# Decoding with a cached 32-head attention and an MLP: wq and wo read as 64 KB rows, x and the heads' results spread over partitions to match, and release signals passed on by waits

## The chip, the cores and the metric

The kernel runs on one core of a Trainium2 chip. Its time is the device time in microseconds of one execution; the number that counts is the median of the runs shown. A profile of one execution is read beside it.

## The reference

One token passes through grouped-query attention over a cache of 65,536 keys and through an MLP, side by side, on the same normalised input. All arrays are float32.

```python
x: (1, 1, 512)   k_cache, v_cache: (1, 8, 65536, 128)
wq: (512, 4096)  wo: (4096, 512)  w1: (512, 1792)  w2: (1792, 512)

xn = layernorm(x)
q = (xn @ wq) as 32 heads of 128          # 4 query heads to each of 8 k/v heads
p = softmax(q @ k.T * 128 ** -0.5)        # over all 65,536 keys
attention = (p @ v) joined @ wo
mlp = relu(xn @ w1) @ w2
return x + attention + mlp
```

The caches hold 268 MB each; wq and wo 8.4 MB each; w1 and w2 3.7 MB each.

## The kernel before, in words

The engines' programs are written out by hand: each engine runs its own list in order, and they meet at semaphores. `Flow.op` waits for the marks it is given, issues an instruction and counts it. Nothing reorders the work.

**Loads.** SyncE issues all large loads on its queue, in this order: wq in two halves of 4 MB (line 149), then for each of 40 steps one part of k (line 158) and one part of v (line 161), then w1 and w2 (lines 164 and 165), then, after the sums over wq, wo in six pieces into the same buffer `big` (lines 268 to 283). There is one buffer for k and one for v. A step is one k/v head and one of five parts of its keys (`PART`: 7, 7, 6, 6 and 6 tiles of 2048 keys). The load of the next k waits until `k_free` has counted the step before, the load of the next v for `v_free`. wq lies in memory head group by head group, so that a partition receives four rows of 8 KB from each half; a piece of wo likewise consists of rows of 8 KB or less. What goes through the helper `load` stands under its line, 142, in the profile. ScalarE issues two small loads on its own queue: x as `xT` (128 rows of 16 B) and x as `x4` (four rows of 512 B).

**Start.** VectorE and TensorE compute the mean and variance and make `xn`. `columns` (line 234) multiplies weights by `xn`: matmuls with one column of weights each, four of them on four groups of 32 rows; VectorE copies the result to `rows`, TensorE transposes it in four blocks, and VectorE picks the columns needed. It runs twice for q, once for each half of wq, and once for the MLP. GpSimd copies one head group's q into `qcur` (line 290) and raises `q_in`.

**A step.** TensorE scores the seven tiles of k into two pairs of PSUM banks `pa` and `pb` (line 307; the seventh tile is also scored where the part has six, and not used). VectorE transposes two tiles at a time into `tr` (line 336); after all of them it drains and raises `k_free` (line 343). Then the maximum, its spread by small matmuls (lines 312 to 314) and `bias`; ScalarE's exponentials into `wt` (line 384); TensorE's 28 matmuls over v into `acc_o` (line 323); and VectorE's addition into `acc`, which raises `v_free` when it is done (lines 357 to 363). The loops of TensorE, VectorE and ScalarE are hardware loops (`Fori`); `head_slot` gives the place in a block of loaded instructions at which a loop's first instruction lies.

**End.** The MLP's first layer, its 14 matmuls over w2 into `acc_z` (line 412), the heads' totals, and the eight matmuls of line 436 that turn the heads' results into `oT`, copied at line 441. Column j of `oT` is head j over its 128 positions, and slice j of `big` is the 128 x 512 piece of wo for that head. 24 slices are summed into `acc_z`, which is copied (line 451) and folded into `acc_y` (line 454); the last eight slices go to `acc_y` in four column blocks (line 463), as their loads arrive. VectorE adds x, and SyncE stores y.

Of the kernel before, what the change touches and what calls it, by code (L numbers as in the profile page):

```python
# [10 lines left out]
ALU = mybir.AluOpType  # L11
AX = mybir.AxisListType
# [9 lines left out]
CT = 4  # L22
# [11 lines left out]
HALF = HKV // 2  # L34
A = D // P
FB = DFF // P
WO = [(0, 4), (4, 2), (6, 1)]
LAST = [(0, 2), (2, 1), (3, 1)]
DIRECT = 6
# [29 lines left out]
def attention_and_mlp_kernel(  # L69
# [21 lines left out]

    nc = tc.nc
# [15 lines left out]
    x4 = place("x4", P)  # L108
    st = place("st", 8)
# [23 lines left out]
    with tc.tile_critical():  # L133
# [6 lines left out]
        def load(engine, name, dst, src, n=16):  # L140
# [6 lines left out]
        tq = big.rearrange("p (h f) -> p h f", h=HKV)  # L147
        wq_in = [
            load(sy, f"wq{i}", tq[:, i : i + HALF, :], wq[i : i + HALF].rearrange("h p a f -> p h (a f)"))
            for i in range(0, HKV, HALF)  # L150
        ]
# [78 lines left out]
        )  # L230
        DV.op(lambda e: e.memset(idg, 1.0))
        DV.op(lambda e: e.tensor_copy(idg[:, :G], ident[:G, :G]), DV.mark)

        def columns(weights, widths, marks, relu=False):


            pr, pt = pa[:, 0, :], pb[:, 0, :]
            DV.op(lambda e: e.memset(pr, 0.0), PE.mark)
            for a in range(A):
                for c, n in enumerate(widths):  # L240
                    PE.op(
                        lambda e: e.matmul(  # L242
                            pr[32 * c : 32 * c + 1, :n], xn[:, a : a + 1], weights(c, a),
                            start=(a == 0), stop=(a == A - 1),
                        ),
                        DV.mark, xn_in, *marks,
                    )
            if relu:
                DV.op(lambda e: e.tensor_scalar_max(rows, pr, 0.0), PE.mark)
            else:  # L250
                DV.op(lambda e: e.tensor_copy(rows, pr), PE.mark)
            for j in range(4):
                PE.op(
                    lambda e: e.transpose(pt[:, j * P : (j + 1) * P], rows[:, j * P : (j + 1) * P], ident),
                    DV.mark, made,
                )
            return pt.rearrange("p (j c l) -> p c j l", j=4, c=CT)[:, :, :, 0]

        for i in range(0, HKV, CT):
            w = tq[:, i : i + CT, :].rearrange("p h (a f) -> p h a f", a=A)  # L260
            q = columns(lambda c, a: w[:, c, a, :], [512] * CT, [wq_in[i // HALF]])
            DV.op(lambda e: e.tensor_copy(qall[:, i : i + CT, :], q), PE.mark)
        q_made, wq_read = DV.mark, PE.mark
# [5 lines left out]
        to = big  # L269
        parts = []  # L270
        wo_in = []
        for h, n in WO:
            mark = load(
                sy, f"wo{h}", to[:, h * 2048 : (h + n) * 2048].rearrange("p (h f) -> p h f", f=2048),
                wo[h : h + n].rearrange("h p g f -> p h (g f)"),
            )
            wo_in += [mark] * (n * G)
        for g, n in LAST:
            at = (HKV - 1) * 2048 + g * D
            mark = load(  # L280
                sy, f"wl{g}", to[:, at : at + n * D], wo[HKV - 1, :, g : g + n, :].rearrange("p g f -> p (g f)")
            )
            wo_in += [mark] * n
# [48 lines left out]
        with nc.Fori(0, HKV, engines=[ENG.DVE], head_slot={ENG.DVE: 0}):  # L332
            for n, nt in enumerate(PART):
                for s in range(0, MOST, 2):
                    w = min(2, MOST - s)
                    i = ve.transpose(  # L336
# [3 lines left out]
                    if s < 4:  # L340
                        i.then_inc(s_dve, 1)
                ve.sem_inc(s_tiles, -4)
                ve.drain().then_inc(k_free, 1)  # L343
# [11 lines left out]
                flat = acc.rearrange("p b d -> p (b d)")  # L355
                if n == 0:
                    i = ve.tensor_copy(flat, acc_o)  # L357
                else:
                    ve.wait_ge(s_alpha, 1).then_inc(s_alpha, -1)
                    i = ve.scalar_tensor_tensor(  # L360
                        flat, flat, alpha[:, n : n + 1], acc_o, op0=ALU.mult, op1=ALU.add
                    )
                i._wait_ge(s_o, 1).then_inc(v_free, 1)
# [13 lines left out]
        with nc.Fori(0, HKV, engines=[ENG.Activation], head_slot={ENG.Activation: 0}):  # L377
# [24 lines left out]
        ends = [min(DFF, 512 * (c + 1)) for c in range(CT)]  # L402
        hid = columns(
            lambda c, a: w[:, a, 512 * c : ends[c]], [ends[c] - 512 * c for c in range(CT)], [w1_in], relu=True
        )
# [35 lines left out]
        oT_in = DV.op(lambda e: e.tensor_copy(oT, pm[:, P : P + HQ]), PE.mark)  # L441

        for j in range(HQ):
            h, g = divmod(j, G)
            row = to[:, j * D : (j + 1) * D]
            lhsT = oT[:, j : j + 1]
            if h < DIRECT:
                gather(g, lhsT, row, [oT_in, wo_in[j]], last=(h == DIRECT - 1))
                if j == DIRECT * G - 1:
# [10 lines left out]
            else:  # L460
                for c in range(CT):
# [3 lines left out]
                            start=False, stop=(j == HQ - 1),  # L465
                        ),
                        oT_in, wo_in[j],
# [34 lines left out]
```

## Time and profile before

| | us |
|---|---|
| median of 3 runs | 1311.38 (1307.83 to 1313.49) |
| the profiled execution, its own time | 1308.58 |
| its span, first to last instruction | 1306.8 |
| TensorE busy | 748.4 |
| VectorE busy | 294.9 |
| ScalarE busy | 88.3 |
| DMA queue of SyncE, share of 16 engines | 99.6% |
| bytes moved | 561.09 MB, 429 GB/s over the span |

Mean granted clock of TensorE: 0.735 of full speed. A busy share is time in which an engine had an instruction under way; loads and their issue are not part of it. "PE", "DVE", "ACT", "POOL" and "SP" are TensorE, VectorE, ScalarE, GpSimd and SyncE; "PEld" is the loading of a matmul's weights. Packets in a DMA queue are the pieces that one DMA engine moves at a time. A float32 matmul leaves two records.

### The profile page before, as it was taken

The page shows a single profiled execution, that of the slowest core. Times are in us where ns is not written, and L with a number is a line of the kernel's source. Part 1 is how long each engine was busy: PE and PEld are TensorE (multiplying, and loading weights), DVE is VectorE, ACT ScalarE, POOL GpSimd, SP SyncE. Part 2 cuts the span into 40 slices and gives each one's busy share as a digit, 9 for nine tenths or more (in the row PEclk, how much of TensorE's full clock was granted, in tenths as well). Part 3 has the DMA queues.
Part 4 walks back from the last instruction along what each step waited for, and adds up shares of the span by engine and source line. Part 5 has one row for each costly group of instructions (what it writes and reads, how often), then busy time and mean ns, then how long its engine had stood idle before and what let it go on. Part 6 is the DMA issues. An engine that isn't in the chain of part 4 may idle for free. (4 is left out here: it accounts for less than half of the span.)

```text
span 1306.8 us, 11612 instructions
## 1 busy us (share of the span) xinstructions
PE 748.4 (57%) x4958; PEld 214.8 (16%) x4958; DVE 294.9 (23%) x474; ACT 88.3 (7%) x372; POOL 4.6 (0%) x22
## 2 busy tenths in 40 slices
PE   4456555556555655556655655556655656555666
PEld 1111111111111111111111111111111111111112
DVE  2122222222212222222222222222221232222221
ACT  0000000000000001000000000000000000100000
POOL 0000000000000000000000000000000000000000
PEclk9667777777767777777766777777766777777778
DMA  9999999999999999999999999999999999999998
GB/s 397 446 427 412 429 433 437 430 427 432 433 435 432 432 436 432 435 429 433 428 441 432 433 433 428 441 425 433 433 435 441 425 433 437 429 442 429 432 425 353
DMA packets 14408, 561.09 MB, mean 429 GB/s; under 512 B 1592, under 2 KB 1600, under 8 KB 1984
## 3 DMA queue, kind: packets, MB, share of 16 engines
q1 hardware_dynamic: 14248, 561.00, 99.6%
q8 instruction: 3, 0.05, 0.0%
q14 instruction: 5, 0.04, 0.0%
q10 hardware_dynamic: 152, 0.00, 0.0%
HBM read 560.99 MB, written 0.00 MB: 429 GB/s over the span
## 5 line engine op out<-in xcount | busy, mean ns | idle before, releaser
L323 PE MATMUL acc_o<-vs,wt 128*16 128x512 f32 x2240 | 328.5, 750 | 128.6 <-PEq L319 128.6
L307 PE MATMUL pa<-ks,qcur 128*32 128x512 f32 x1280 | 220.1, 820 | 285.8 <-PEq L302 285.8
L336 DVE STREAM_TRANSPOSE tr<-pa 128x1024 f32<-128x1024 f32 x80 | 100.0, 1250 | 404.2 <-PE pa L307 404.2
L307 PE MATMUL pb<-ks,qcur 128*32 128x512 f32 x960 | 139.3, 685 | 0.0
L323 PEld LDWEIGHTS acc_o<-vs,wt 128*16 128x16 f32 x2240 | 76.4, 114 | 347.2 <-issue 347.2
L384 ACT ACTIVATE wt<-tr,bias 128x96 f32<-128x96 f32 (+1 forms) x160 | 73.1, 465 | 875.5 <-ACTq L379 875.5
L307 PEld LDWEIGHTS pa<-ks,qcur 128*32 128x32 f32 x1280 | 48.6, 134 | 420.0 <-issue 409.1
L360 DVE SCALAR_TENSOR_TENSOR acc<-acc,alpha,acc_o 128x512 f32<-128x512 f32 x32 | 23.9, 747 | 348.8 <-PE acc_o L323 348.8
L336 DVE STREAM_TRANSPOSE tr<-pb 128x1024 f32<-128x1024 f32 x80 | 76.9, 962 | 38.0 <-PE pb L307 38.0
L312 PE MATMUL pm<-ident,m 128*4 128x128 f32 x40 | 11.5, 286 | 90.0 <-DVE m L348 73.0
L307 PEld LDWEIGHTS pb<-ks,qcur 128*32 128x32 f32 x960 | 41.2, 138 | 110.5 <-issue 86.6
L313 PE MATMUL pm<-dg,ones 4*128 4x4 f32 x80 | 21.6, 338 | 26.7 <-DVE dg L352 26.7
L384 ACT ACTIVATION_READ_ACCUMULATOR wt<-tr,bias 128x1 f32 x160 | 29.9, 187 | 0.0
L357 DVE COPY acc<-acc_o 128x512 f32<-128x512 f32 x8 | 5.5, 691 | 102.9 <-PE acc_o L323 102.9
L345 DVE TENSOR_REDUCE mc<-tr 128x4 f32<-128x384 f32 (+1 forms) x32 | 26.2, 819 | 3.7
L312 PEld LDWEIGHTS pm<-ident,m 128*4 128x4 f32 x40 | 3.3, 81 | 126.3 <-DVE m L348 102.0
L313 PEld LDWEIGHTS pm<-dg,ones 4*128 4x128 f32 x80 | 18.1, 280 | 34.9 <-DVE dg L352 34.9
L314 PE MATMUL pm<-dg,rowg 4*128 4x1 f32 x80 | 21.6, 337 | 0.0
L314 PEld LDWEIGHTS pm<-dg,rowg 4*128 4x128 f32 x80 | 20.6, 313 | 0.0
L382 ACT COPY wt<-zero 128x64 f32<-128x64 f32 x8 | 2.0, 244 | 232.5 <-ACTq L379 232.5
L242 PE MATMUL pa<-big,xn 128*1 128x512 f32 x64 | 11.5, 888 | 10.0 <-DMA big<-wq 10.0
L353 DVE COPY bias<-pm 128x5 f32<-128x5 f32 x40 | 6.5, 164 | 41.5 <-PE pm L314 41.5
(83 smaller groups left out, 115.3 us busy)
## 6 DMA issues: line engine op xcount, KB each, us to landing
ks<-k SPq DMA_DIRECT2D x24, 6144.0 KB, 19.8
vs<-v SPq DMA_DIRECT2D x24, 6144.0 KB, 19.4
ks<-k SPq DMA_DIRECT2D x16, 7168.0 KB, 23.5
vs<-v SPq DMA_DIRECT2D x16, 7168.0 KB, 24.3
big<-wq SPq DMA_DIRECT2D x2, 4096.0 KB, 17.2
ks<-w SPq DMA_DIRECT2D x2, 3584.0 KB, 17.7
big<-wo SPq DMA_DIRECT2D x1, 4096.0 KB, 31.4
big<-wo SPq DMA_DIRECT2D x1, 2048.0 KB, 35.9
```

Of the source, the lines that this page charges most:

```text
L242: lambda e: e.matmul(pr[32 * c : 32 * c + 1, :n], xn[:, a : a + 1], weights(c, a), start=(a == 0), stop=(a == A - 1),),
L307: i = te.matmul(pt[32 * c : 32 * c + 32, :], qcur, ks[:, at : at + TW], start=True, stop=True)
L312: te.transpose(pm[:G, :P], m, ident)._wait_ge(s_dve, 3).then_inc(s_max, 1)
L313: te.matmul(pm[:, P : P + G], ones[:G, :], dg[:, :G], start=True, stop=True)._wait_ge(s_dve, 4)
L314: te.matmul(pm[:, P + G : P + G + 1], rowg, dg[:, G : G + 1], start=True, stop=True).then_inc(s_max, 1)
L323: mm = te.matmul(acc_o[32 * c : 32 * c + WIDE * G, :], wt[:, i * WIDE : (i + 1) * WIDE, :].rearrange("p b g -> p (b g)"), vs[:, i * 512 : ...
L336: i = ve.transpose(tr[:, s * SUB : (s + w) * SUB, :].rearrange("p b i -> p (b i)"), (pa, pb)[s // 2 % 2][:, :w, :].rearrange("p i k -> p ( ...
L345: i = ve.reduce_max(top, tr[:, : nt * SUB, :G].rearrange("p b g -> p g b"), axis=AX.X)
L353: ve.tensor_copy(bias[:, n, :], pm[:, P : P + G + 1])._wait_ge(s_max, 2).then_inc(s_bias, 1)
L357: i = ve.tensor_copy(flat, acc_o)
L360: i = ve.scalar_tensor_tensor(flat, flat, alpha[:, n : n + 1], acc_o, op0=ALU.mult, op1=ALU.add)
L384: i = se.activation(wt[:, : nt * SUB, g], tr[:, : nt * SUB, g], AF.Exp, bias=bias[:, n, g : g + 1], scale=scale, accum_out=part[:, n, g : ...
```

## The change

- wq is read in one load: partition p receives the 64 KB that lie at p times 64 KB. Its 128 partitions are then 8 head groups times 16 row blocks, and a slice of `big` holds, for partition (h, i), row `(i, r)` of head group h. For this x is loaded a second time as `xr`, by ScalarE's queue: 32 values of x in each partition, the same 16 blocks for each of 8 head groups. VectorE normalises `xr` and multiplies it by `mine`, which is 1 where a partition belongs to a head group, giving `xs` with eight columns to each slice (in `tr`'s memory). 32 matmuls with eight columns of weights follow in one go; after the four transposes one reduction makes `qall` for all heads.
- wo is read in the same order, as pieces of 16, 8, 4, 2, 1 and 1 slices of a 64 KB row. Behind `oT`, VectorE makes `pick` (in `tr`'s memory), eight matmuls spread `oT` over the partitions, and a product with `mine` and a reduction give `sw`, whose column j goes with slice j.
- `k_free` is raised by a wait of VectorE for `s_tiles`, once the tiles are scored that the following k load will overwrite; `v_free` by a wait for `s_o`, ahead of the addition into `acc`.
- The loops' heads lie at slot 128 (VectorE) and 68 (ScalarE); TensorE's stays at 0.

```diff
--- before.py
+++ after.py
@@ -31,12 +31,12 @@
 NP = len(PART)
 STEPS = HKV * NP
 WIDE = 4
-HALF = HKV // 2
 A = D // P
 FB = DFF // P
-WO = [(0, 4), (4, 2), (6, 1)]
-LAST = [(0, 2), (2, 1), (3, 1)]
-DIRECT = 6
+R = HKV
+SLICES = R * G
+WO = [16, 8, 4, 2, 1, 1]
+DIRECT = 24
 EPS = 1e-5
 
 
...
@@ -106,6 +110,13 @@
     wt = place("wt", MOST * SUB, G)
     xT, xc, sq, xn = (place(n, A) for n in ("xT", "xc", "sq", "xn"))
     x4 = place("x4", P)
+    xr, sw = place("xr", SLICES), place("sw", SLICES)
+    mine = place("mine", HKV)
+
+    flat_tr = tr.rearrange("p b i -> p (b i)")
+    xs = flat_tr[:, : SLICES * HKV].rearrange("p (i h) -> p i h", h=HKV)
+    pick = flat_tr[:, : R * P].rearrange("p (r q) -> p r q", r=R)
+    spread = flat_tr[:, R * P : R * (P + HQ)].rearrange("p (r h g) -> p r h g", r=R, h=HKV)
     st = place("st", 8)
     ident, ones = place("ident", P), place("ones", P)
     sel, selb, selg = place("sel", WIDE, G), place("selb", WIDE), place("selg", G)
@@ -144,11 +155,10 @@
 
 
         x_in = load(se, "x_in", xT, x.rearrange("(p a) -> p a", p=P))
-        tq = big.rearrange("p (h f) -> p h f", h=HKV)
-        wq_in = [
-            load(sy, f"wq{i}", tq[:, i : i + HALF, :], wq[i : i + HALF].rearrange("h p a f -> p h (a f)"))
-            for i in range(0, HKV, HALF)
-        ]
+        wq_in = load(sy, "wq_in", big, wq.rearrange("h (i r) a f -> (h i) (r a f)", r=R))
+        xr_in = load(
+            se, "xr_in", xr, x.rearrange("(i j) -> i j", j=SLICES).unsqueeze(0).to_broadcast([HKV, P // R, SLICES])
+        )
         for i in range(STEPS):
             h, n = divmod(i, NP)
             lo, nt = sum(PART[:n]), PART[n]
@@ -228,59 +238,58 @@
                 rowg.rearrange("g (i j) -> g i j", j=G), ident[:G, :G].unsqueeze(1).to_broadcast([G, P // G, G])
             )
         )
+        DV.op(lambda e: e.reduce_sum(mine, ident.rearrange("p (h i) -> p h i", h=HKV), axis=AX.X))
+        DV.op(lambda e: e.tensor_scalar(xr, xr, st[:, 1:2], None, op0=ALU.subtract), xr_in)
+        DV.op(lambda e: e.tensor_scalar_mul(xr, xr, st[:, 7:8]), DV.mark)
+        xs_in = DV.op(
+            lambda e: e.tensor_mul(
+                xs, xr.unsqueeze(2).to_broadcast([P, SLICES, HKV]),
+                mine.unsqueeze(1).to_broadcast([P, SLICES, HKV]),
+            ),
+            DV.mark,
+        )
         DV.op(lambda e: e.memset(idg, 1.0))
         DV.op(lambda e: e.tensor_copy(idg[:, :G], ident[:G, :G]), DV.mark)
 
-        def columns(weights, widths, marks, relu=False):
-
-
-            pr, pt = pa[:, 0, :], pb[:, 0, :]
-            DV.op(lambda e: e.memset(pr, 0.0), PE.mark)
-            for a in range(A):
-                for c, n in enumerate(widths):
-                    PE.op(
-                        lambda e: e.matmul(
-                            pr[32 * c : 32 * c + 1, :n], xn[:, a : a + 1], weights(c, a),
-                            start=(a == 0), stop=(a == A - 1),
-                        ),
-                        DV.mark, xn_in, *marks,
-                    )
-            if relu:
-                DV.op(lambda e: e.tensor_scalar_max(rows, pr, 0.0), PE.mark)
-            else:
-                DV.op(lambda e: e.tensor_copy(rows, pr), PE.mark)
+        pr, pt = pa[:, 0, :], pb[:, 0, :]
+
+        def clear():
+            return DV.op(lambda e: e.memset(pr, 0.0), PE.mark)
+
+        def turn():
+
             for j in range(4):
                 PE.op(
                     lambda e: e.transpose(pt[:, j * P : (j + 1) * P], rows[:, j * P : (j + 1) * P], ident),
                     DV.mark, made,
                 )
-            return pt.rearrange("p (j c l) -> p c j l", j=4, c=CT)[:, :, :, 0]
-
-        for i in range(0, HKV, CT):
-            w = tq[:, i : i + CT, :].rearrange("p h (a f) -> p h a f", a=A)
-            q = columns(lambda c, a: w[:, c, a, :], [512] * CT, [wq_in[i // HALF]])
-            DV.op(lambda e: e.tensor_copy(qall[:, i : i + CT, :], q), PE.mark)
-        q_made, wq_read = DV.mark, PE.mark
+            return pt.rearrange("p (j c l) -> p j c l", j=4, c=CT)
+
+        cleared = clear()
+        for i in range(SLICES):
+            c = i % CT
+            PE.op(
+                lambda e: e.matmul(
+                    pr[32 * c : 32 * c + HKV, :], xs[:, i, :], big[:, i * 512 : (i + 1) * 512],
+                    start=(i < CT), stop=(i >= SLICES - CT),
+                ),
+                cleared, xs_in, wq_in,
+            )
+        wq_read = PE.mark
+        DV.op(lambda e: e.tensor_copy(rows, pr), PE.mark)
+        q = turn()[:, :, :, :HKV].rearrange("p j c h -> p h j c")
+        DV.op(lambda e: e.reduce_sum(qall, q, axis=AX.X), PE.mark)
+        q_made = DV.mark
         PE.need(DV.mark)
         AC.need(DV.mark)
 
 
         sy.wait_ge(*wq_read)
-        to = big
-        parts = []
         wo_in = []
-        for h, n in WO:
-            mark = load(
-                sy, f"wo{h}", to[:, h * 2048 : (h + n) * 2048].rearrange("p (h f) -> p h f", f=2048),
-                wo[h : h + n].rearrange("h p g f -> p h (g f)"),
-            )
-            wo_in += [mark] * (n * G)
-        for g, n in LAST:
-            at = (HKV - 1) * 2048 + g * D
-            mark = load(
-                sy, f"wl{g}", to[:, at : at + n * D], wo[HKV - 1, :, g : g + n, :].rearrange("p g f -> p (g f)")
-            )
-            wo_in += [mark] * n
+        flat_wo = wo.rearrange("h (i r) g f -> (h i) (r g f)", r=R)
+        for n in WO:
+            cut = slice(len(wo_in) * D, (len(wo_in) + n) * D)
+            wo_in += [load(sy, f"wo{len(wo_in)}", big[:, cut], flat_wo[:, cut])] * n
 
 
         ge.wait_ge(*q_made)
@@ -329,18 +338,24 @@
             mm.then_inc(s_o, 1)
 
 
-        with nc.Fori(0, HKV, engines=[ENG.DVE], head_slot={ENG.DVE: 0}):
+        with nc.Fori(0, HKV, engines=[ENG.DVE], head_slot={ENG.DVE: 128}):
             for n, nt in enumerate(PART):
+
+                follow = PART[(n + 1) % NP]
                 for s in range(0, MOST, 2):
                     w = min(2, MOST - s)
+                    if s < follow <= s + 2 and follow == MOST:
+                        ve.wait_ge(s_tiles, s // 2 + 1).then_inc(k_free, 1)
                     i = ve.transpose(
                         tr[:, s * SUB : (s + w) * SUB, :].rearrange("p b i -> p (b i)"),
                         (pa, pb)[s // 2 % 2][:, :w, :].rearrange("p i k -> p (i k)"),
                     )._wait_ge(s_tiles, s // 2 + 1)
                     if s < 4:
                         i.then_inc(s_dve, 1)
+                    if s < follow <= s + 2 and follow < MOST:
+                        ve.wait_ge(s_tiles, s // 2 + 1).then_inc(k_free, 1)
                 ve.sem_inc(s_tiles, -4)
-                ve.drain().then_inc(k_free, 1)
+                ve.drain()
                 top = m if n == 0 else mc
                 i = ve.reduce_max(top, tr[:, : nt * SUB, :G].rearrange("p b g -> p g b"), axis=AX.X)
                 if n:
@@ -353,14 +368,15 @@
                 ve.tensor_copy(bias[:, n, :], pm[:, P : P + G + 1])._wait_ge(s_max, 2).then_inc(s_bias, 1)
                 ve.sem_inc(s_max, -2)
                 flat = acc.rearrange("p b d -> p (b d)")
+                if n:
+                    ve.wait_ge(s_alpha, 1).then_inc(s_alpha, -1)
+                ve.wait_ge(s_o, 1).then_inc(v_free, 1)
                 if n == 0:
-                    i = ve.tensor_copy(flat, acc_o)
+                    ve.tensor_copy(flat, acc_o)
                 else:
-                    ve.wait_ge(s_alpha, 1).then_inc(s_alpha, -1)
-                    i = ve.scalar_tensor_tensor(
+                    ve.scalar_tensor_tensor(
                         flat, flat, alpha[:, n : n + 1], acc_o, op0=ALU.mult, op1=ALU.add
                     )
-                i._wait_ge(s_o, 1).then_inc(v_free, 1)
                 ve.sem_inc(s_o, -1)
             ve.drain()
             last = bias[:, NP - 1, :G].unsqueeze(1).to_broadcast([P, NP - 1, G])
@@ -374,7 +390,7 @@
             ve.reduce_sum(fin[:, :DH], masked.rearrange("p b d -> p d b"), axis=AX.X).then_inc(f_out, 1)
 
 
-        with nc.Fori(0, HKV, engines=[ENG.Activation], head_slot={ENG.Activation: 0}):
+        with nc.Fori(0, HKV, engines=[ENG.Activation], head_slot={ENG.Activation: 68}):
             for n, nt in enumerate(PART):
                 se.wait_ge(s_bias, 1).then_inc(s_bias, -1)
                 if n and nt < PART[n - 1]:
@@ -399,10 +415,19 @@
 
         PE.need(GP.mark)
         w = t1.rearrange("p (a f) -> p a f", a=A)
-        ends = [min(DFF, 512 * (c + 1)) for c in range(CT)]
-        hid = columns(
-            lambda c, a: w[:, a, 512 * c : ends[c]], [ends[c] - 512 * c for c in range(CT)], [w1_in], relu=True
-        )
+        cleared = clear()
+        for a in range(A):
+            for c in range(CT):
+                lo, hi = 512 * c, min(DFF, 512 * (c + 1))
+                PE.op(
+                    lambda e: e.matmul(
+                        pr[32 * c : 32 * c + 1, : hi - lo], xn[:, a : a + 1], w[:, a, lo:hi],
+                        start=(a == 0), stop=(a == A - 1),
+                    ),
+                    cleared, xn_in, w1_in,
+                )
+        DV.op(lambda e: e.tensor_scalar_max(rows, pr, 0.0), PE.mark)
+        hid = turn()[:, :, :, 0].rearrange("p j c -> p c j")
         DV.op(lambda e: e.tensor_copy(hT.rearrange("p (c j) -> p c j", c=CT), hid), PE.mark)
         begun = set()
 
@@ -438,15 +463,39 @@
                 ),
                 DV.mark,
             )
-        oT_in = DV.op(lambda e: e.tensor_copy(oT, pm[:, P : P + HQ]), PE.mark)
-
-        for j in range(HQ):
-            h, g = divmod(j, G)
-            row = to[:, j * D : (j + 1) * D]
-            lhsT = oT[:, j : j + 1]
-            if h < DIRECT:
-                gather(g, lhsT, row, [oT_in, wo_in[j]], last=(h == DIRECT - 1))
-                if j == DIRECT * G - 1:
+        DV.op(lambda e: e.tensor_copy(oT, pm[:, P : P + HQ]), PE.mark)
+        DV.op(
+            lambda e: e.tensor_copy(
+                pick.rearrange("p r (h i) -> p r h i", h=HKV),
+                ident.rearrange("p (i r) -> p r i", r=R).unsqueeze(2).to_broadcast([P, R, HKV, P // R]),
+            )
+        )
+        pz = pb[:, 1, :]
+        for r in range(R):
+            PE.op(
+                lambda e: e.matmul(pz[:, r * HQ : (r + 1) * HQ], pick[:, r, :], oT, start=True, stop=True),
+                DV.mark,
+            )
+        DV.op(
+            lambda e: e.tensor_mul(
+                spread, pz[:, : R * HQ].rearrange("p (r h g) -> p r h g", r=R, h=HKV),
+                mine.unsqueeze(1).unsqueeze(3).to_broadcast([P, R, HKV, G]),
+            ),
+            PE.mark,
+        )
+        sw_in = DV.op(
+            lambda e: e.reduce_sum(
+                sw.rearrange("p (r g) -> p r g", r=R), spread.rearrange("p r h g -> p r g h"), axis=AX.X
+            ),
+            DV.mark,
+        )
+
+        for j in range(SLICES):
+            row = big[:, j * D : (j + 1) * D]
+            lhsT = sw[:, j : j + 1]
+            if j < DIRECT:
+                gather(j % CT, lhsT, row, [sw_in, wo_in[j]], last=(j >= DIRECT - CT))
+                if j == DIRECT - 1:
 
                     DV.op(lambda e: e.tensor_copy(rows, acc_z), PE.mark)
                     for c in range(CT):
@@ -462,9 +511,9 @@
                     PE.op(
                         lambda e: e.matmul(
                             acc_y[32 * c : 32 * c + 1, :P], lhsT, row[:, c * P : (c + 1) * P],
-                            start=False, stop=(j == HQ - 1),
+                            start=False, stop=(j == SLICES - 1),
                         ),
-                        oT_in, wo_in[j],
+                        sw_in, wo_in[j],
                     )
         DV.op(lambda e: e.tensor_add(x4, acc_y[:, :P], x4), PE.mark, x4_in)
         sy.wait_ge(*DV.mark)
```

## The prediction

> **What bounds the kernel now.** I read the page's slices and queues first, then the stretches of the start, then the chain and the order of events at both ends.
>
> ```profile
> span 1306.8 us, 11612 instructions
> PE 748.4 (57%) x4958; PEld 214.8 (16%) x4958; DVE 294.9 (23%) x474; ACT 88.3 (7%) x372; POOL 4.6 (0%) x22
> DMA  9999999999999999999999999999999999999998
> ...
> q1 hardware_dynamic: 14248, 561.00, 99.6%
> ...
> q10 hardware_dynamic: 152, 0.00, 0.0%
> ...
> ks<-k SPq DMA_DIRECT2D x24, 6144.0 KB, 19.8
> vs<-v SPq DMA_DIRECT2D x24, 6144.0 KB, 19.4
> ```
>
> Queue q1 (SP's) fills the 16 DMA engines for 99.6% of the span; no compute engine is above 57%. A load of 6144 KB lands 19.4 to 19.8 us after its issue, though 6.29 MB at the 432 GB/s of the middle slices take 14.6 us: each is issued about 5 us before the one ahead of it ends. So the kernel is a stream of 561 MB; only bytes, rate, holes in the stream, and what lies before and after it count.
>
> The stretches of wq, the first k and the first v (columns: us, busy time and count per engine, granted clock, DMA share, GB/s), and the time order around them:
>
> ```profile
> 2.10:22.90 20.80, 8.38 (x40) 2.45 (x40) 5.87 (x27) 2.97 (x4) 0.00 (x0) 1.00 1.08 442
> 22.90:39.90 17.00, 5.65 (x36) 1.27 (x36) 0.86 (x2) 0.00 (x0) 0.19 (x1) 0.70 1.00 427
> ```
> ```profile
> 1.39 1.09 ACTq L142 DMA_DIRECT2D x<-x  x1
> ...
> 13.62 6.55 PE L242 MATMUL pa<-big,xn 128*1 128x512 f32 x32 [8.16 <-DMA big<-wq]
> ...
> 23.57 5.00 PE L242 MATMUL pa<-big,xn 128*1 128x512 f32 x32 [1.84 <-DMA big<-wq]
> ...
> 42.73 3.64 PE L307 MATMUL pa<-ks,qcur 128*32 128x512 f32 x16 [12.61 <-PEq L302]
> ...
> 52.09 0.33 SPq L158 DMA_DIRECT2D ks<-k  x1
> ```
>
> q is done by 30.7 (POOL's copy), 12 us before the first k is complete at 42.7. The next k is issued at 52.09, when the first is used up; the first v covers the stream until 56.9 to 59.4. That cover, 5 to 7 us, is what a late q would eat.
>
> The DMA queues in 5.85 to 6.15 us and in 6.15 to 6.45 us (packets, MB, share):
>
> ```profile
> q1 hardware_dynamic: 16, 0.13, 104.3%
> q10 hardware_dynamic: 4, 0.00, 2.2%
> ```
> ```profile
> q1 hardware_dynamic: 16, 0.13, 103.4%
> q10 hardware_dynamic: 4, 0.00, 0.8%
> ```
>
> This is the small load of x into x4 (q10 is ACT's queue) beside wq. Its four rows move in the first window, its four completion writes in the second, and between them each of the 16 engines starts one 8 KB packet of wq. So the two queues take turns packet by packet, and the small load waited from its issue's end at 2.48 to 5.9. The 152 packets of q10 are 144 for the 128-row load of x (128 rows, 16 completions) plus 4 + 4: a load whose outer dimension is 4 ran on four engines only.
>
> **The change, part by part.**
>
> *wq in 64 KB rows.* 8.39 MB took 20.8 us in 8 KB packets. The first k, in 57,344 B packets, moved 7.34 MB in 17.0 us; at that rate wq takes 19.4, plus some 0.4 to start: 1.0 us less. Bounds 0 and 1.4. One engine's packet now lasts 17.0/8 = 2.12 us for k and 2.42 us for wq.
>
> *xr, the new small load.* x goes to 128 rows of 128 B from a source with outer dimension 8. By the 4-row load I take 8 engines, each with 16 rows and a completion: 17 packets, each taking turns with one q1 packet. ACT issues it at 1.4, and after the 1.09 us of the 4-row issue its packets reach the engines when wq's first is running. The 4-row load let 74 KB (2.8 us beyond the 0.6 us that x's first load needed) pass ahead; here that is about wq's second row. Then each of xr's 17 packets waits for one more q1 packet, the last of them for the 18th: wq's 8 and its completion, k's 8 and its completion. So xr lands when the first k does, at 39.9 - 1.0 + 0.3 (17 switches of some 0.02) = 39.2. Bounds: 24 if 16 engines share it, 10 if its rows go in one turn, 43.5 if two more packets pass ahead.
>
> *q behind it.* VectorE: two 128x32 operations at 0.2, the product 128x256 at 0.45 (between 0.17 for 16 columns and 0.68 for 512), idg's two at 0.3, the clear 0.5, small gaps: 1.7, so TensorE starts at 40.9. It has the 64 matmul records in one go: 6.55 + 5.00 = 11.6 with two cold starts, 9.4 with one (24 cold records at 0.214, 40 at 0.107): 50.3. Copy of rows, transposes, the reduction into qall and POOL's copy took 2.1 after the second half; with a wider reduction 2.3: 52.6 instead of 30.7. The wait on xr holds idg and the clear behind it on VectorE, for which nobody else waits. ACT's extra issue moves its table load by 1.1, inside the 1.9 us that it waited for VectorE.
>
> *The hole.* Scoring took 8.26 (42.73 to 50.99), of it 1.7 from the cold clock; I take 7.5: 60.1. The passed-on signal gives the issue at 60.2 (the old one would come 1.0 later). From issue to first packet 1.1 (wq: 0.96 to 2.1), 0.4 to start: the stream flows from 61.7. It ran dry at 55.9 + 0.3. Before, it flowed on from 56.9, but the slowest engine, which sets every landing, was 59.4 there and 1265.8 at the last v (issue 1246.66 + 19.1). From 61.7 the same 522 MB need about 1207.5 at 432.5 GB/s: 1269.2 or 1269.3, so the last v is **3.5 us later**. The second v (first v used up at 52.6 + 26 = 78.6, less 0.7) is issued just ahead of the second k's end at 78.7, so no second hole over 1 us. Each of xr's turns may also delay the following k packet: 0 by the 8 KB packets after the 4-row load, up to 1.2 us by what two k packets lost after instruction packets at 35.3. Seventeen times that is 0 to 20; nearest is the plain load, I take **+1.0**.
>
> *Signals passed on, loop heads.* k's signal comes 1.0 earlier, v's 0.75 earlier; with issues some 5 us ahead the stream cannot use it (0 to -0.4). Instructions loaded at the loops' heads were hidden by the wait for k: 0.
>
> *The end.* In the order of time:
>
> ```profile
> 1291.89 0.19 DVE L441 COPY oT<-pm 128x32 f32<-128x32 f32 x1 [2.04 <-PE pm L436]
> ...
> 1293.03 6.86 PE L412 MATMUL acc_z<-big,oT 128*1 128x512 f32 x48 [1.18 <-DMA big<-wo]
> ...
> 1302.95 0.40 PE L463 MATMUL acc_y<-big,oT 128*1 128x128 f32 x8 [0.23 <-DMA big<-wo]
> ```
>
> TensorE waits only 1.2 us for the first piece of wo, 0.3 for the second, 0.23 for the last: compute and stream end nearly together. Between oT and the sums now stand pick (128x1024: 1.2, between two 512 memsets 0.97 and two 512 copies 1.4), eight matmuls with full weights (L436's eight: 1.95), spread 128x256 (0.45), its reduction (0.55, between 0.19 for 20 and 0.79 for 384 columns), gaps 0.3: 4.5, of which 1.1 was waiting for wo. The other two waits (0.55) vanish, and a warm clock may give 0.4: **+2.4**, bounds 1.0 and 3.5. wo's own saving (its 8 KB and smaller packets, about 0.6) is off the path then.
>
> **Sum.** 3.5 + 1.0 + 2.4 = +6.9 on the profiled run's own 1308.58: 1315.5. The median of the runs, 1311.38, is 2.8 above that run: **1318.3**.
>
> **Rivals.** *xr lands early* (not slower). If its 16 rows pass in one turn (10 us), or 16 engines take 8 each (24 us), or wq's rows are cut into 32 KB packets (about 25), q is ready by 40 and the first k, complete by 41.7, covers it. Then -1.0 - 0.3 + 2.4 = +1.1: 1312.5. It decides at xr landing before about 28 us. Against it speaks the order of rows and completions in the two windows; for it, that a multi-row load beside a busy queue isn't shown. The Trainium skill ("DMA: Bandwidth & Descriptors", Queues, rings and completion order) says that an engine drains a whole packet, typically 9 to 17 descriptors, from one ring before it switches; by that rule the sum would be this rival's. The trace's rows and completions with single 8 KB packets between them speak for one descriptor per turn. The same page (Why a DMA increments its semaphore by 16 and not by 1) gives the number of engines as the largest up to 16 dividing both outer sizes, so 8 here; the four engines for four rows agree.
>
> *Turns that cost.* If each turn holds the next k packet by half of the 1.2 us, eight engines lag by 10 us instead of 1.0: 1327.
>
> *The end is hidden.* If the clock stays high and pick is cheap, the end costs 1.0 and the first case gives 1317; the hole still decides.
>
> **How the numbers follow.** xr late as worked out: 62%, +6.9 with about 3 either way (landing at 37 to 43.5, the end's bounds). xr early: 28%. Costly turns: 10%. No-change bound 0.5% is 6.6 us, about what a measurement here can tell: the first case is just above it, 55% slower. Slower: 0.34 + 0.10 + noise; same: 0.28 of the first plus most of the early case; faster needs over 6.6 us from a stream with no holes. Range 1309.5 (early case with the end at 1.0 and no other loss) to 1327; the likeliest case alone 1315 to 1322.
>
> **What would show it.** Right: q10 packets spread from 3 to about 40 us, the q matmuls starting near 41, the second k issued near 60, a slice with low GB/s at 56 to 62, sums over wo starting 3 us later after oT with no wait for the last wo. Wrong: q matmuls starting at 22 to 25, with full DMA slices.

## The result and the profile after

The changed kernel takes 1331.18 us (median of 6 runs, 1325.07 to 1335.65) beside 1309.97 for the kernel before on the same chip: a ratio of 1.0155, 95% interval 1.013 to 1.018. So it is 21 us slower. The six runs lie in two groups: 1325.07, 1328.14 and 1328.44, and 1333.91, 1334.91 and 1335.65. The profiled execution is the fastest of them (1325.07, span 1322.9), 16.5 above the profiled execution of before.

Bytes, slices and the two queues on the page of the changed kernel:

```profile
span 1322.9 us, 11719 instructions
...
DMA  9699999999999999999999999999999999999996
GB/s 415 284 430 433 437 424 444 424 428 438 433 442 428 430 428 440 440 427 435 422 444 428 428 438 430 444 431 430 428 436 442 426 438 425 437 432 428 435 429 255
...
q1 hardware_dynamic: 12824, 561.00, 98.2%
...
q10 hardware_dynamic: 288, 0.02, 0.0%
```

The same line of before:

```profile
GB/s 397 446 427 412 429 433 437 430 427 432 433 435 432 432 436 432 435 429 433 428 441 432 433 433 428 441 425 433 433 435 441 425 433 437 429 442 429 432 425 353
```

The same 561 MB; the second slice (33 to 66 us) has 284 GB/s instead of 446. The other slices, the last apart, are near those of before: the stream lost its time in one place near the start, and something at the end. The start in the order of time:

```profile
0.93 0.42 ACTq L153 DMA_DIRECT2D xT<-x  x1
...
0.96 0.40 SPq L153 DMA_DIRECT2D big<-wq  x1
...
1.38 1.25 ACTq L153 DMA_DIRECT2D xr<-x  x1
...
13.45 0.16 DVE L206 TENSOR_REDUCE st<-xT 128x1 f32<-128x4 f32 x1 [10.16 <-DMA xT<-x]
...
46.33 0.24 DVE L242 TENSOR_SCALAR xr<-xr,st 128x32 f32<-128x32 f32 x1 [27.84 <-DMA xr<-x]
...
48.17 8.39 PE L272 MATMUL pa<-big,tr 128*8 128x512 f32 x64 [32.44 <-DVE pa L257]
...
58.59 0.19 POOL L299 COPY qcur<-qall 128x4 f32<-128x4 f32 x1 [56.91 <-DVE qall L281]
...
65.59 0.33 SPq L168 DMA_DIRECT2D ks<-k  x1
```

VectorE waits for `xr` until 46.3, the q matmuls start at 48.2, and the second k is issued at 65.6 instead of 52.1. The stretch of 10 us that the stream then lacks, in the changed kernel and in the kernel before (columns as in the prediction's stretches):

```profile
57.00:67.00 10.00, 6.87 (x60) 2.43 (x60) 5.43 (x7) 0.00 (x0) 0.19 (x1) 1.00 0.26 84
```
```profile
57.00:67.00 10.00, 7.30 (x52) 1.85 (x56) 0.00 (x0) 0.37 (x2) 0.00 (x0) 0.65 0.87 378
```

84 GB/s, where before 378 GB/s flowed. A second thing stands in the start's lines, which the prediction did not have: even `xT`, the 2 KB load issued ahead of all, was complete only at 13.4 (VectorE had waited for it 10.16 us). In before VectorE used it without a wait:

```profile
3.19 0.15 DVE L196 TENSOR_REDUCE st<-xT 128x1 f32<-128x4 f32 x1
```

The two queues of the changed kernel in four stretches, 5 to 8, 10 to 12, 12 to 14 and 14.5 to 17 us (packets, MB, share):

```profile
q1 hardware_dynamic: 29, 1.90, 146.1%
q10 hardware_dynamic: 29, 0.00, 0.5%
...
q1 hardware_dynamic: 13, 0.85, 98.2%
q10 hardware_dynamic: 13, 0.00, 0.4%
...
q1 hardware_dynamic: 16, 1.05, 120.9%
q10 hardware_dynamic: 16, 0.00, 0.5%
...
q1 hardware_dynamic: 16, 1.05, 96.7%
q10 hardware_dynamic: 8, 0.00, 0.3%
```

29 small packets go with 29 packets of 64 KB, 13 with 13, 16 with 16: the engines alternate one for one. Up to 14 us these are `xT`'s rows, and in the third stretch its 16 completions, one to an engine. Only behind those, in the last stretch, `xr`'s rows begin: 16 engines move a wq packet each, and eight of them one row of `xr`. By 14.5 us 80 packets of wq have started, five to each engine, and no row of `xr`.

The end, in the order of time:

```profile
1302.39 0.19 DVE L466 COPY oT<-pm 128x32 f32<-128x32 f32 x1 [2.04 <-PE pm L461]
1302.50 1.07 DVE L468 COPY tr<-ident 128x1024 f32<-128x1024 f32 x1
1303.62 3.62 PE L476 MATMUL pb<-oT,tr 128*128 128x32 f32 x16 [1.27 <-DVE tr L468]
1307.28 0.42 DVE L480 TENSOR_TENSOR tr<-pb,mine 128x256 f32<-128x256 f32 x1 [3.71 <-PE pb L476]
1307.74 0.60 DVE L487 TENSOR_REDUCE sw<-tr 128x32 f32<-128x256 f32 x1
1308.40 8.01 PE L437 MATMUL acc_z<-big,sw 128*1 128x512 f32 x48 [1.16 <-DVE sw L487]
...
1317.53 1.93 PE L512 MATMUL acc_y<-big,sw 128*1 128x128 f32 x64
```

`oT` is 10.5 us later than before (1302.39 against 1291.89); from `oT` to the sums over wo are 6.0 us instead of 1.1, the sums take 8.01 instead of 6.86, and no wait for wo is left. From `oT` to the store of y are 17.5 us instead of 11.9 (issued at 1319.92; 1303.82 before), so 5.6 of the 16.1 by which the span is longer lie behind `oT`, and 10.5 ahead of it. The granted clock is in the stretches of L461, the spread (L476) and the sums (L437):

```profile
1300.40:1302.40 2.00, 1.95 (x16) 1.86 (x16) 0.01 (x1) 0.00 (x0) 0.00 (x0) 1.00 1.00 426
...
1303.60:1307.30 3.70, 3.62 (x16) 3.49 (x16) 0.02 (x1) 0.00 (x0) 0.00 (x0) 0.50 0.96 401
1308.40:1316.50 8.10, 8.01 (x48) 1.36 (x48) 0.00 (x0) 0.00 (x0) 0.00 (x0) 0.66 0.22 80
```

Sixteen records with full weights took 1.95 us at a clock of 1.00 (four columns each, L461) and 3.62 at 0.50 (32 columns each, L476).

### The profile page after: what moved, and what is told of

Its sections match the earlier page's. It is cut to its first block, busy times and chain, and to the rows that moved or that the text cites. A ratio compares the mean times of both kernels' runs of the same rounds, so it can differ in the third digit from the quotient of the medians.

```text
span 1322.9 us, 11719 instructions
## 1 busy us (share of the span) xinstructions
PE 742.3 (56%) x4970; PEld 216.3 (16%) x4970; DVE 297.0 (22%) x478; ACT 88.3 (7%) x372; POOL 4.5 (0%) x22
## 5 line engine op out<-in xcount | busy, mean ns | idle before, releaser
L272 PE MATMUL pa<-big,tr 128*8 128x512 f32 x64 | 8.4, 684 | 32.4 <-DVE pa L257 32.4
## 6 DMA issues: line engine op xcount, KB each, us to landing
vs<-v SPq DMA_DIRECT2D x16, 7168.0 KB, 25.1
ks<-w SPq DMA_DIRECT2D x2, 3584.0 KB, 17.5
```

Of the source, the lines that this page charges most:

```text
L272: lambda e: e.matmul(pr[32 * c : 32 * c + HKV, :], xs[:, i, :], big[:, i * 512 : (i + 1) * 512], start=(i < CT), stop=(i >= SLICES - CT),),
```

## The experiments

The theory from this profile: (1) `xr` is late because its rows take turns with wq's packets, and everything else at the start follows; (2) the end costs 4 to 6 us, and the clock is in it. Rivals: the eight-column matmuls, the 64 KB rows themselves, or the moved signals.

**One part alone.** *start_only* is before with the new start (one wq load, `xr`, eight-column matmuls), and the old signals, heads and end. *end_only* is before with the new order of wo, `pick`, the spread and `sw`.

> The kernel before with the new start alone: wq in one load of 64 KB rows, xr behind it on ScalarE's queue, 32 matmuls with eight columns. Turns theory (xr's 16 rows on each of eight engines alternate with packets of 64 and 57 KB): xr lands at 44 to 50 us, the stream has a hole of about 10 us near 57 to 67, and the time is 8 to 14 us above before; the runs scatter by several us as those of the changed kernel do. End theory (most of the 21 us comes from the extra work behind oT): not more than 3 us above before.

> The kernel before with the new end alone: wo in 64 KB rows, pick, spread, sw. Turns theory: no hole, every load until the last v as before, 6 to 8 us slower, all of it after the last v; the runs agree within 4 us. End theory: 15 to 20 us slower.

start_only: 1324.97 (1319.22 to 1331.06), 1.0123 (1.0077 to 1.0169), 14.8 us above before and so just above its 8 to 14, with `xr` at 46.1 and the runs in two groups again (1319.22 and 1320.23; 1329.71 and 1331.06). end_only: 1314.59 (1313.47 to 1317.42), 1.0033 (1.0021 to 1.0045), so 4.5 us, below its 6 to 8. Most of the loss, and the two groups, are in the start.

**xr ahead of wq.** *xr_first* is the changed kernel with one load moved:

```diff
+        xr_in = load(sy, "xr_in", xr, ...)
         wq_in = load(sy, "wq_in", big, ...)
-        xr_in = load(se, "xr_in", xr, ...)
```

> The changed kernel with xr issued on SyncE's queue ahead of wq. Turns theory: xr lands before 4 us, the q matmuls start at 23 to 25 us, when wq is complete, qcur is made before the first k lands, no hole; time before + 5 to 8 us, all at the end. One-pass theory (q is late because all of wq and 64 matmul records in one go stand ahead of it, wherever xr is): the hole of about 10 us stays, and the time is that of the changed kernel.

1314.84 (1313.93 to 1315.58), 1.0032 (1.0019 to 1.0044). The q matmuls are bound by wq again, and the stream has no hole:

```profile
24.11 8.32 PE L272 MATMUL pa<-big,tr 128*8 128x512 f32 x64 [18.64 <-DMA big<-wq]
...
34.45 0.19 POOL L299 COPY qcur<-qall 128x4 f32<-128x4 f32 x1 [32.78 <-DVE qall L281]
```

So 16 us of the loss are the place of one 16 KB load. The eight-column matmuls and the 64 KB rows by themselves are not the cause, since both are still there. `xT` is through early here too (used at 3.19); wq goes out at 1.80 instead of 0.96. The time is 4.7 us above before, just below the 5 to 8 expected.

**The size of a turn.** *wq_8k* is the changed kernel with the same bytes of wq in eight loads of 8 KB rows; `xr` stays behind it on ScalarE's queue.

```diff
-        wq_in = load(sy, "wq_in", big, wq.rearrange("h (i r) a f -> (h i) (r a f)", r=R))
+        flat_wq = wq.rearrange("h (i r) a f -> (h i) (r a f)", r=R)
+        wq_in = [
+            load(sy, f"wq{r}", big[:, r * 2048 : (r + 1) * 2048], flat_wq[:, r * 2048 : (r + 1) * 2048])
+            for r in range(R)
+        ]
```

> The changed kernel with wq read into the same places by eight loads of 8 KB rows, xr where the change has it. Turns theory: a turn lasts 0.31 to 0.33 us beside wq, so xr lands at 8 to 15 us, the q matmuls wait for wq at 23 to 26 us, no hole; before + 6 to 9 us. One-pass theory: hole and time as in the changed kernel.

1314.69, 1.0035 (1.0022 to 1.0048), so 4.6 us above before, less than the 6 to 9 expected. `xr` took turns here too, but short ones:

```profile
11.32 0.24 DVE L246 TENSOR_SCALAR xr<-xr,st 128x32 f32<-128x32 f32 x1 [1.79 <-DMA xr<-x]
```

`xr` is used at 11.3 behind 8 KB packets and at 46.3 behind 64 KB ones: the wait goes with the length of the packets that it takes turns with.

**When the small loads are issued.** *x_late* holds ScalarE's two loads until `x4` is cleared (`xT` issued at 1.39, `xr` at 1.83). *x_sp* gives `xT` to SyncE, ahead of wq. *x_split* does that too, and holds `xr` until `zero` is cleared:

```diff
--- x_late
-        x_in = load(se, "x_in", xT, ...)
         wq_in = load(sy, "wq_in", big, ...)
-        xr_in = load(se, "xr_in", xr, ...)
...
         se.wait_ge(*x4_free)
+        x_in = load(se, "x_in", xT, ...)
+        xr_in = load(se, "xr_in", xr, ...)
--- x_sp
-        x_in = load(se, "x_in", xT, ...)
+        x_in = load(sy, "x_in", xT, ...)
--- x_split, beside x_sp's line
-        xr_in = load(se, "xr_in", xr, ...)
...
         d = memset(DV, zero, 0.0)
+        zero_made = DV.mark
...
         se.wait_ge(*x4_free)
+        se.wait_ge(*zero_made)
+        xr_in = load(se, "xr_in", xr, ...)
```

> The changed kernel with ScalarE's two loads of x (xT and xr) held until VectorE has cleared x4, about 0.5 us later, so that wq's packets are there first. Turns theory: now xT's 8 rows on each engine take turns too, before xr's 16; xr lands when SyncE's stream has run dry, at 55 to 58 us, the hole grows to about 20 us, and the runs agree at 1332 to 1337 us: the slower of the two groups in which the changed kernel's runs lie. If 0.5 us of issue order does not matter: 1325 to 1335 us, as the changed kernel.

> The changed kernel with xT issued by SyncE ahead of wq, xr left on ScalarE's queue. Turns theory: one turn fewer (xT's completion is out of the way), xr lands at 41 to 45 us, the hole is 6 to 9 us, the runs agree within 4 us at 1320 to 1326 us: the two groups become one. If the groups have another cause than x's rows meeting wq's: two groups 5 to 10 us apart again.

> The changed kernel with xT issued by SyncE ahead of wq (it lands at 3.2 us there) and ScalarE's xr held until VectorE has cleared `zero`, so issued at about 1.5 us, 0.1 after wq instead of 0.04 before it. xr should again meet wq's packets and land between 41 and 57 us, against 3.35 with the issue at 0.92. If the scatter of the changed kernel's runs (1323 to 1336) comes from where xT's rows fall among wq's packets, all runs of this kernel lie within 0.4% of each other, at 1318 to 1334 by the landing; if xr's own rows cause it, two groups some 10 us apart are here too.

x_late: 1333.46 (1331.23 to 1338.85), 1.0184 (1.0161 to 1.0207). Its four runs do not agree as closely as expected: they spread over 7.6 us. Its loads met wq 0.45 us later, and `xT` was complete at 25.1, `xr` at 57.2, when the stream had run dry:

```profile
25.11 0.16 DVE L206 TENSOR_REDUCE st<-xT 128x1 f32<-128x4 f32 x1 [21.82 <-DMA xT<-x]
...
57.24 0.24 DVE L242 TENSOR_SCALAR xr<-xr,st 128x32 f32<-128x32 f32 x1 [27.08 <-DMA xr<-x]
...
76.56 0.33 SPq L164 DMA_DIRECT2D ks<-k  x1
```

x_sp missed its expectation (`xr` at 41 to 45 us): 1314.72, 1.0032 (1.0019 to 1.0045), as with `xr` first. ScalarE now issued `xr` as its first instruction, at 0.92, while wq went out at 1.42, so that the rows were through before wq's (used at 8.16). In x_split, with `xr` issued at 1.57, 0.15 after wq, the hole is back, in the size of the prediction:

```profile
1.42 0.41 SPq L153 DMA_DIRECT2D big<-wq  x1
1.57 1.26 ACTq L153 DMA_DIRECT2D xr<-x  x1
...
40.53 0.24 DVE L244 TENSOR_SCALAR xr<-xr,st 128x32 f32<-128x32 f32 x1 [32.30 <-DMA xr<-x]
60.08 0.33 SPq L165 DMA_DIRECT2D ks<-k  x1
```

Its time is 1318.08 (1317.08 to 1318.94, 5 runs), 1.0064 (1.005 to 1.0078). Without `xT` in the race `xr` is used at 40.5 instead of 46.3, and the runs agree within 0.15%. The packets say why. Here 32 packets of wq, two to each engine, have started when the first row of `xr` moves, at 8.04; in the changed kernel 80, five to each engine, when it moves at 14.66. The four turns just before that, from 4.98 on, are `xT`'s: three rows and a completion on each engine. So `xT`, which precedes `xr` in its queue, takes turns first. The changed kernel also issued `xr` 0.42 us after wq, and x_split 0.15 after it; since `xT`'s turns fill the whole time up to `xr`'s first row, that difference does not show in the landing.

The changed kernel profiled twice more (*after_b*, *after_c*):

> The changed kernel once more, for a profile of another execution. Turns theory: the time goes with the time at which xr lands. An execution near 1326 us has xT complete at 12 to 14 us and xr at 46; one near 1334 us has xT complete at 20 to 26 us and xr at 54 to 58. If the slower group has another cause, xr lands at 46 in both.

> As after_b: about 1326 us with xr landing near 46 us, or about 1334 us with xr landing at 54 to 58 us.

1324.43 and 1323.15, both with `xr` used at 46.4. The longer group was never profiled, so the half of these expectations that is about it stays untested. It lies at x_late's time, whose `xr` came at 57, and it is gone where `xT` is out of the race; that it is a later place of `xT`'s rows among wq's is the likely reading, not shown.

**The end.** *xr_first_old_end* is xr_first with the end of before. *end_pick_fill* is xr_first with `pick` made earlier (behind `hT`) and four matmuls whose result is not used ahead of the spread and of the sums. *fill_long* is xr_first with 32 such matmuls ahead of the spread, and none ahead of the sums:

```diff
+        def fill():
+            for c in range(CT):
+                PE.op(lambda e: e.matmul(pa[32 * c : 32 * c + 1, 1, :], xn[:, 0:1], vs[:, c * D : (c + 1) * D],
+                                         start=True, stop=True))
+        for _ in range(8):
+            fill()
         pz = pb[:, 1, :]
```

> xr issued by SyncE ahead of wq, wq in 64 KB rows, passed-on signals and loop heads as changed, and the end as before (wo in heads' order, no pick, spread, sw). By the terms found so far: start 0 to -1, end 0, signals 0: 0.1% faster to equal, 1308 to 1311 us.

> xr_first with pick copied earlier, behind hT, and with four filler matmuls into an unused bank ahead of the spread matmuls and four ahead of the sums over wo; their results are not used. Clock theory (the new end costs more than its instructions because TensorE's pauses and weight loads leave the granted clock at 0.5 from the spread matmuls on): clock 1.0 in the spread, which takes 2.0 us instead of 3.6, sums over wo in 5 to 6.5 us instead of 7.8, 3 to 4 us faster than xr_first. If the spread's matmuls are slow for another reason (32 columns of oT): 3.6 us again and less than 1.5 us gained, by pick alone.

> xr_first with 32 filler matmuls of 512 columns into an unused bank ahead of the spread matmuls, results not used. If the spread's eight matmuls take 3.6 us because of the granted clock: the clock is 1.0 by their start and they take 1.9 to 2.1 us. If because of their 32 columns: 3.6 us at clock 1.0 as well. The fillers themselves cost 4 to 8 us.

xr_first_old_end: 1307.97 (11 runs, 1307.52 to 1309.01), 0.9982 (0.9973 to 0.9991), so 0.2% faster than before, and 6.9 us below xr_first, which ran on another chip (6.6 by the two ratios). end_pick_fill: 1313.38, 1.0022 (1.0013 to 1.0032), 1.5 us below xr_first on another chip, with intervals that overlap. It did not do what the clock theory expected: the clock was 1.00 during the four fillers ahead of the spread, but 0.52 in the spread, which took 3.55. That left open whether the 32 columns make the spread slow. fill_long, run once (1317.46), gains no time since its fillers take 8.72 us, but it settles this. The spread and the sums of xr_first, the spread of end_pick_fill, and the spread and the sums of fill_long:

```profile
1293.48 3.62 PE L476 MATMUL pb<-oT,tr 128*128 128x32 f32 x16 [1.27 <-DVE tr L468]
...
1298.26 7.81 PE L437 MATMUL acc_z<-big,sw 128*1 128x512 f32 x48 [1.15 <-DVE sw L487]
```
```profile
1294.10 3.55 PE L485 MATMUL pb<-oT,tr 128*128 128x32 f32 x16
```
```profile
1300.37 1.97 PE L486 MATMUL pb<-oT,tr 128*128 128x32 f32 x16
...
1303.49 5.33 PE L437 MATMUL acc_z<-big,sw 128*1 128x512 f32 x48 [1.15 <-DVE sw L497]
```

Behind 32 fillers, at a clock of 1.00, the spread takes 1.97 us instead of 3.62, and the sums 5.33 instead of 7.81. So the low clock, and not the 32 columns, makes the spread slow, and it takes some 4 us of the new end (1.65 and 2.48). Not all of that is new: in before, too, the sums over wo began at a clock of 0.50 (1293.0 to 1296.1) and took 6.86. Of what the end costs more than before, the clock explains some 2.6 to 2.8 us (1.65, and 0.95 to 1.15 in the sums); the rest is mostly the added work between `oT` and the sums. What lowers the clock just ahead of the spread is not shown.

**Signals and heads.** *signals_only* is before with the passed-on signals and the moved loop heads; *signals_no_heads* and *heads_only* take one each.

```diff
--- heads_only
-        with nc.Fori(0, HKV, engines=[ENG.DVE], head_slot={ENG.DVE: 0}):
+        with nc.Fori(0, HKV, engines=[ENG.DVE], head_slot={ENG.DVE: 128}):
...
-        with nc.Fori(0, HKV, engines=[ENG.Activation], head_slot={ENG.Activation: 0}):
+        with nc.Fori(0, HKV, engines=[ENG.Activation], head_slot={ENG.Activation: 68}):
```

> The kernel before with the passed-on signals and the new loop heads alone. Since loads are issued some 5 us before the stream needs them: the next k is issued about 1 us earlier after the scores, and the time is equal within 0.1%. If the signals matter to the stream: 0.3% or more faster.

> The kernel before with the passed-on signals alone, the loops' heads at slot 0 as before. Signals and heads together gave -2 us. If the earlier signals close the small dry spots of the stream, this kernel has the 1308 of both, and the dry spots near 120 and 150 us are gone; if the loading of instructions at the loops' heads made them, it has the 1310.2 of the kernel before.

> The kernel before with the loops' heads moved alone (VectorE to slot 128, ScalarE to slot 68), the signals as before. By the theory that the signals gave the 2 us: 1310.2, as before, within 0.6. By the theory of the heads: 1308.

signals_only: 1308.25 (10 runs), 0.9979 (0.9969 to 0.9989), against its expectation of no difference. Apart, 1308.69 and 0.9992 (0.9983 to 1.0001), and 1309.21 and 0.9996 (0.9987 to 1.0005): neither is told from no change, their sum (1.6 us) is near the 2.0 of both, and which of them carries it stays open. The dips of the stream that signals_no_heads was to remove did not go: it has 279 GB/s at 118 to 121 us (before 311), and 524 and 295 at 146 to 149 and 149 to 152 (before 344 and 393). What the signals do is seen in the landings of the k loads, of signals_no_heads and then of heads_only:

```profile
ks<-k SPq DMA_DIRECT2D x24, 6144.0 KB, 21.6
...
ks<-k SPq DMA_DIRECT2D x24, 6144.0 KB, 19.8
```

With the signals a load lands 1.8 us later after its issue, at the same mean rate of the stream (430 and 427 GB/s), which fits an issue that is so much earlier. With the heads alone it stays at the 19.8 of before.

## Why the prediction was wrong

The forecast time lay above before, and the kernel did become slower, but the chances were about even: 0.34 and 0.10 for slower, and 0.28 with most of another 0.28 for no change. The time was 12.9 us above the forecast and outside the range. Counted from before the miss is larger: 6.9 us were forecast and 21.2 came. (The 2.8 us that the forecast added for the median went with a median of three runs, 1311.38; that of six is 1309.97.)

*Where xr's turns begin: the step that failed.* "Here that is about wq's second row", with 39.2 as the landing. The count of what goes ahead had only wq's packets in it, two to an engine. It left out `xT`, which ScalarE issues just before on the same queue: with wq's first packets at 64 KB its last three rows on each engine and its completions now take turns too, up to 13.4 us, and `xr`'s rows come behind them, so that five packets of wq went ahead on each engine. In before wq went out at the same moment, but its packets were short, and `xT` was used at 3.19 without a wait. Measured: used at 46.3, above the bound of 43.5, which had two more packets ahead of it. With `xT` out of the way, in x_split, two packets of wq go ahead as counted, `xr` is used at 40.5, and the second k goes out at 60.08 (60.2 was forecast). That its time is 1318.08, where 1318.3 was forecast, is in part luck: the end cost more than forecast, the signals gained, and before was lower. With `xT` gone from the race, and wq issued 0.46 us later, 13 of the 21 us go (1331.18 to 1318.08): some 7 against the execution of the result's profile, where `xT`'s turns are seen, and 16 to 18 against the longer group, whose cause is not shown.

*The form of the turns held.* Eight engines, 16 rows and a completion each: x_split's ScalarE queue has 144 packets, 136 of `xr` and 8 of `x4`, and the rows come in groups of eight with 16 packets of wq. The rule of the Trainium skill ("DMA: Bandwidth & Descriptors", Queues, rings and completion order) that a whole packet of typically 9 to 17 descriptors is drained before an engine switches would have let the 16 rows pass in one turn; the stretches with 29 and 29, and 13 and 13 packets show one descriptor to a turn in these loads. That rival is refuted.

*The cost of a switch, +1.0.* No such loss is seen. In the records of the packets `xr`'s groups of eight come 2.42 us apart beside wq and 2.12 beside k, which is the length of one such packet. In x_split the forecast 3.5 for the hole, -1.9 for the signals and 6.9 for the end behind the new start make 8.5, and 8.3 were measured (1318.08 - 1309.77). Costly turns, the third case, would have shown there too.

*From xr to the issue.* 21.0 us were forecast (39.2 to 60.2), 19.3 came (46.3 to 65.6): q matmuls 8.39 instead of 9.4, and 6.8 from `qcur` to the issue instead of 7.6, at a granted clock of 1.00 (57 to 67 us).

*The hole.* Forecast 5.8 us with the last v 3.5 later; in x_split the second k came as forecast, and the matmuls over the last v start 2.9 us later than before (1268.95; 1266.09). In the changed kernel, with `xr` 5.8 us later than there, the second k is issued 5.5 later, and the last v's matmuls start 9.2 later than before (1275.33).

*wq's 64 KB rows, -1.0.* xr_first_old_end has them without the hole, and its ratio, 0.9982, is not told from the 0.9979 of signals_only: no gain is seen, and the term is near its bound of 0. It was read from the rate of one stretch.

*The end, +2.4, bounds 1.0 and 3.5.* The end alone costs 4.5 us (end_only), and 6.6 to 6.9 behind the new start without hole; with their intervals the two are not told apart. `pick` was priced rightly (1.2; 1.07), and the matmuls wrongly: 1.95 for the spread was L436's price at a clock of 1.00, and here the clock was 0.50 (3.62); and 0.4 was hoped for from "a warm clock", where the sums came out 1.15 slower. The Trainium skill ("TensorE: Matmul & The Clock Gate", What's actually happening) has the clock fall to half after an idle window of about 3.4 us and return after a busy one. The trace agrees on the half (1.00 at L461, 0.50 at the spread) and fill_long on the return; but the pauses ahead of the spread were only 0.68 and 1.27 us, with small matmuls between them, and no run here shows why the clock fell.

*Signals, 0 to -0.4.* About -2. "With issues some 5 us ahead the stream cannot use it" was argued from the median landing; the runs with both parts show that the kernel gains; by which of them is open.

Together: 14.8 for the start, 4.5 for the end and -1.9 for the signals are 17.3, against 21.2 measured; start_only's median, between two groups of two, is good to some 6 us. The lower end of the range does not follow from its terms: 1311.38 - 1.0 - 0.3 + 1.0 is 1311.1, not 1309.5.

## What to carry to other kernels

A small load that met a stream of large rows waited here for one large packet to each of its own rows and to its completion (2.42 us beside wq's, 2.12 beside k's). So its landing can be estimated as rows per engine, plus one, times the packet's length, and what stands ahead of it in its own queue counts in the same way. Put small loads that a start depends on ahead of the stream, on the stream's own queue where the order must hold: here `xr` issued 0.50 us ahead of wq was there when wanted, at 8.2, and issued 0.15 behind it came at 40.5. Where a change puts work of another engine between two runs of matmuls, look up the granted clock of the matmuls behind it and price the matmuls with it: here 0.50, and 3.62 us instead of 1.97.

## What was not expected of the hardware

- A 2 KB load issued 0.03 us ahead of a stream of 64 KB rows took until 13.4 us; 0.46 us later, until 25.1. With 8 KB rows beside it (before) it was used at 3.19.
- The changed kernel's runs, and start_only's, fall in two groups some 8 to 11 us apart by their means, and those of x_split and of xr_first do not (spreads of 0.14% and 0.13%). Since the longer group was not profiled, it is not shown that the race of issue between the two queues makes the groups.
- Four matmuls of 512 columns ahead of a spread did not keep the clock up (0.52 in the spread, 3.55 us); behind 32 it was 1.00 (1.97).
